# Two heads share one set of softmax sums, and the last head's last tile moves from TensorE to VectorE

## The chip, the cores and the metric

The kernel runs on one core of a Trainium2 chip. The metric is the device time of one execution in microseconds (us). The kernel before takes 1801.33 us, the median of three runs (1801.32, 1801.33 and 1802.16 us). The engines are called by the profile's names: PE is TensorE (matrix products), PEld its loading of weights, DVE is VectorE, ACT is ScalarE, POOL is GpSimd and SP is SyncE. SP and POOL, and now and then ACT, also issue the DMA transfers; "SPq" and "POOLq" are their queues of instructions. An engine takes its instructions strictly in order.

## The reference, cut to what matters

The program computes two branches on the same tokens (2048 tokens of width 1024) and mixes them with a gate, `g * a + (1 - g) * b`. Branch `b` is PEER, a mixture of 64 small experts whose output is a sum over rows of a table `v`. Branch `a` is attention with 32 heads of width 32, and that is where the change lies:

```python
scores = jnp.einsum("bhqd,bhkd->bhqk", q, k) * (Dh ** -0.5)
p = _softmax(scores, axis=-1)
o = jnp.einsum("bhqk,bhkd->bhqd", p, v)
return (lambda x, *d: x.transpose(*d))(o, 0, 2, 1, 3).reshape(B, S, D) @ wo
```

The softmax needs, for each head and each of the 2048 queries, the sum of the exponentials over the 2048 keys. The kernel computes the product with `v` from the exponentials as they are, and divides by that sum later.

## The kernel before, in words

Up to about 600 us the kernel computes queries, keys, values and PEER's choice of experts. Then comes the attention, to about 1622 us, and last the product with `wo`, which also adds PEER's values.

In the attention the keys of a head are cut into NT = 16 tiles of 128 keys. A tile `P[h, kt]` has 128 partitions (keys) and 2048 columns (queries) of float32, 1 MB in all; there are eight such buffers, used in turn. A step number counts tiles: step = 16 * h + kt. The main loop (lines 1536 to 1551) takes two steps at once. For each pair it issues, in this order: `scores` (L1346), eight matmuls into a ring of seven PSUM banks, and ACT's exponentials of them (L1356); `pv` (L1367), the products of the pair of tiles before with the values; and then, for each of the two steps, first the work that the table `todo` has for that step (entered with `at(step, function, ...)`, lines 1501 to 1532) and then `presum`. So the order on each engine is written out by hand, and every engine's instructions keep it.

The sum over the keys is made in three ways:

- `presum` (L1384 to L1396) adds most tiles of a head on DVE into an accumulator `ACC[h]` (128 x 2048).
- The tiles in `SUMS[h]` (L1376) go another way. The first of them is written by ACT directly into a second accumulator `ACCD[h]` (the buffer `accd`) instead of a P buffer. For each of the others POOL issues a DMA that adds the 1 MB tile to `ACCD[h]` in memory (L1389). All of a head's DMA additions write the same buffer, and each carries a wait for the one before. `merge` (L1399) then adds `ACCD[h]` to `ACC[h]` on DVE.
- What is left is a sum over the 128 partitions, which `rowsum` (L1380) does on PE as products with ones: four matmuls of 32 x 512, one for each quarter of the queries. In the profile an fp32 matmul of this kind counts as two instructions, so a set of four is "x8".

Heads 0 to 27 (NP = 28) are first folded by two DMAs from 128 to 32 partitions (`fold_half`, L1404, and `fold_quarter`, L1407), and four heads are gathered into one buffer, so that four heads share one set of four matmuls (`group_sums`). Heads 28, 29 and 30 have a set of their own each (`head_sums`), at steps 29*16+8, 30*16+8 and 31*16+8. Head 31 is summed behind the loop: two sets, one over its last tile `P[31, 15]`, which never goes into `ACC`, and one over `ACC[31]` after the last `merge`. These two stand on PE behind the first part of the product with `wo` (`wo_mm(pa, 0, [0], ...)`, L1581, 12 matmuls) and ahead of its other parts.

The buffers tie steps together. `ACC[28]` is `acc1`, which `ACC[31]` uses next (L1394 of head 31). `ACC[29]` is the buffer `vhl`, into which `load_vhl` loads PEER's table (two DMAs of 512 KB on SP) once head 29's sums are done; the table is first used at L1588, at 1643 us. Behind the loop the P buffers become buffers of the product with `wo`. The sums go out through `SMD`, come back as `rr`, are inverted (L1452), and reach the last chunk of the attention's output by L1650.

Of the kernel before, what the change touches and what calls it, by code (L numbers as in the profile page):

```python
# [9 lines left out]
F32 = mybir.dt.float32  # L10
F32R = mybir.dt.float32r
I32 = mybir.dt.int32
AF = mybir.ActivationFunctionType
OP = mybir.AluOpType
# [4 lines left out]
H = 32  # L19
KC = D // 128  # L20
HC = KC // 2
NT = S // 128
NQ = S // 512
G = H // 4
# [7 lines left out]
def gated_mha_peer_kernel(ctx, tc, xT, wqkv, wv, wo, wq, k12, ug, v, out):  # L32
# [8 lines left out]
    nc = tc.nc  # L41
# [3 lines left out]
    const = ctx.enter_context(tc.tile_pool(name="const", bufs=1))  # L45
# [12 lines left out]
    SMD = [dram.tile([4, S], F32, name=f"smd{g}") for g in range(G)]  # L58
# [11 lines left out]


    gw = const.tile([128, KC, 1], F32, name="gw")
    const.tile([128, 112], F32, name="fill")
    ctx.enter_context(tc.tile_pool(name="fillr", bufs=1, side="right")).tile([128, 120], F32, name="fillr")

    def dma(dst, src, queue=nc.sync):
        a, b = (ap.bitcast(F32) if ap.dtype == F32R else ap for ap in (dst, src))
        return queue.dma_start(a, b)  # L78
# [636 lines left out]
    sm = Pool("sm")  # L715
# [501 lines left out]
    P, pools = {}, {}  # L1217
# [48 lines left out]
    NP = H - 4  # L1266
    ACC = {}

    def new_acc(h):
        if h % 3 == 2 and h < H - 2:  # L1270
            ACC[h] = keep.tile([128, S], F32, name="vhl")
        else:
            ACC[h] = wk.tile([128, S], F32, name=f"acc{h % 3 if h < H - 2 else h % 2}", bufs=1)
# [6 lines left out]
    def raw_wo(kc):  # L1280
        i, j = divmod((kc - 1) % KC, 2)
        return wo_raw[i][:, j]

    wk = Pool("wk", bufs=2)
# [3 lines left out]
    nc.vector.memset(sel, 0.0)  # L1288
    for i in range(4):
        nc.vector.memset(sel[32 * i:32 * i + 32, i:i + 1], 1.0)  # L1290
    vpool = Pool("vpool", bufs=2)
    kq = Pool("kq")
    pools["left"] = Pool("ppl")
# [7 lines left out]
    ring = pss.tile([128, NB, 512], F32, name="ring")  # L1301
# [3 lines left out]
    def ring_banks(n):  # L1305
        i = [(ring_no[0] + k) % NB for k in range(n)]
        ring_no[0] += n
        return i

    def on_ring(ins, *banks):  # L1310

        for other, theirs in users:
            if ins.ins.engine != other.ins.engine and not theirs & set(banks):
                tc.declare_no_dep(ins.ins, other.ins, reason="different banks of the ring")
        users.append((ins, set(banks)))
        del users[:-6 * NB]
# [18 lines left out]
    def scores(tiles):  # L1335
# [7 lines left out]
        for c, i in enumerate(banks):  # L1343
# [6 lines left out]
            q0, m = c0 % NQ, c + 1 - c0  # L1350
            if q0 == 0 and kt == SUMS[h][0]:
                P[h, kt] = ACCD[h] = wk.tile([128, S], F32, name="accd")
# [19 lines left out]

    SUMS = {h: (1, 3, 8, 12) for h in range(H)} | {h: (1, 4, 10) for h in range(1, NP, 2)} | {0: (4, 8, 12), H - 1: (2, 4, 6, 11)}

    def rowsum(ps, *srcs, by=ones):
        for src in srcs:
            for qc in range(NQ):
                yield nc.tensor.matmul(ps[32 * qc:32 * qc + 32, :], by,  # L1380
                                       src[:, qc * 512:(qc + 1) * 512],
                                       start=(src is srcs[0]), stop=(src is srcs[-1]))

    def presum(h, kt):  # L1384
        sums = SUMS[h]
        if kt == 0 or kt == sums[0] or (h == H - 1 and kt == NT - 1):
            return
        if kt in sums:
            nc.gpsimd.dma_start(ACCD[h], P[h, kt], accum_op=OP.add)  # L1389
            return  # L1390
        if kt == 1 + (sums[0] == 1):
            if h > 0:
                new_acc(h)
            nc.vector.tensor_add(ACC[h], P[h, 0], P[h, kt])  # L1394
        else:
            nc.vector.tensor_add(ACC[h], ACC[h], P[h, kt])  # L1396

    def merge(h):
        nc.vector.tensor_add(ACC[h], ACC[h], ACCD[h])  # L1399
# [15 lines left out]
    def group_sums(g):  # L1415
        i, = ring_banks(1)
        for ins in rowsum(ring[:, i, :], F.pop(g), by=sel):
            on_ring(ins, i)
        o = wk.tile([128, 512], F32, name="ssb")
        on_ring(nc.scalar.activation(o, ring[:, i, :], AF.Copy), i)  # L1420
        for j in range(4):
            dma(SMD[g][j:j + 1, :].rearrange("o (q s) -> (o q) s", q=NQ), o[j::32, :])

    def head_sums(h):
        i, = ring_banks(1)
        for ins in rowsum(ring[:, i, :], ACC.pop(h)):
            on_ring(ins, i)
        on_ring(norm_sums(h, ring[:, i, :]), i)
# [69 lines left out]
    def at(step, f, *a):  # L1498
        todo.setdefault(step, []).append((f, a))

    for h in range(H):
        base = h * NT
        g, j = divmod(h, 4)
        if h < H - 1:
            at(base + NT, finish, h)
            at(base + NT + 5, merge, h)
            if h >= NP:
                at(base + NT + 8, head_sums, h)
            else:
                at(base + NT + 9, fold_half, h)  # L1510
                at(base + 2 * NT + 4, fold_quarter, h)
                at(base + 2 * NT + 8, gather, h)
                if j == 3:
                    at(base + 2 * NT + 14, group_sums, g)
        if j == 3 and g + 1 < G:
            at(base + 3 * NT + 4, load_r, g)
            at(base + 3 * NT + 8, norm_r, g)
        if h >= 1 and h + 1 < H:
            at(base + 2, load_head, h + 1)
        if g + 1 < G:  # L1520
            at(base + 7, load_v, g + 1, j)
    for i, step in enumerate((6, 7, 9, 11)):
        at((H - 1) * NT + step, split_first, i)
    for k in range(2 * KC):
        c = slice(k % 2 * D // 2, (k % 2 + 1) * D // 2)
        at((8 + k) * NT + 11, dma, raw_wo(k // 2)[:, c], wo_rows[:, :, k // 2 * D:(k // 2 + 1) * D][:, :, c])
    for i in range(2):
        at(30 * NT + 9 + i, load_vhl, i)
    at(29 * NT + 13, load_o, 0, 0, 4)
    at(30 * NT + 7, load_o, 0, 4, KC - 1)  # L1530
    at(30 * NT + 13, load_rb, 0, 0, KC - 1)
# [4 lines left out]
    for b0 in range(0, (H + 1) * NT, BT):  # L1536
        if b0 > H * NT:
            break
        now = [divmod(k, NT) for k in range(b0, b0 + BT)] if b0 < H * NT else []
        if now:  # L1540

            if b0:
                scores(now)
        for k in range(b0 - BT, b0):
            if k >= 0:
                pv(*divmod(k, NT))
        for k in range(b0, b0 + BT):
            for f, a in todo.pop(k, []):
                f(*a)
            if now:  # L1550
                presum(*now[k - b0])
    assert not todo
    merge(H - 1)
    pss.close()
    pools["left"].close()
    pools["right"].close()
# [47 lines left out]
    def split_hi(kc):  # L1604
        nc.scalar.activation(woh[kc], raw_wo(kc), AF.Copy)
        if kc < KC - 1:
            o = OC[0][:, kc, :]
            nc.vector.tensor_mul(o, o, RB[0][:, kc, :])
            nc.scalar.activation(OH[0][:, kc, :], o, AF.Copy)
# [52 lines left out]
    load_o(1, 0, KC - 1)  # L1662
    load_t(2, [zp.tile([128, S], F32R, name="z1")], [fin.tile([128, S], F32R, name="t3l")])
    sm = pso.tile([128, 512], F32, name="o")
    list(rowsum(sm, P[H - 1, NT - 1], ACC.pop(H - 1)))
    split_hi(1)
    for kc in range(1, KC - 1):
        split_hi(kc + 1)
# [167 lines left out]
```

## Time and profile before

| | us |
|---|---|
| median of three runs | 1801.33 |
| the profiled execution, its own time | 1799.57 |
| span of that execution, first to last instruction | 1797.7 |
| PE busy in the span | 1791.9 (100%) |
| DVE busy | 1505.5 (84%) |
| ACT busy | 1303.6 (73%) |
| POOL busy | 265.4 (15%) |

The profile shows one execution; all places are given in us from the start of its span. Rows of a timeline have start, duration, engine, line, operation, "written<-read", and the number of instructions merged into the row; in brackets stand the idle time ahead of the first of them and what ended it. Busy PE is not PE at its peak, since matmuls overlap. DMAs are named by the instruction that issues them; where the profile knows it, "DMA to landing" is the time from the issue to the last byte's semaphore.

Step numbers are found in the trace by counting pairs of steps back from the last eight score matmuls at 1616.24 us (steps 510 and 511). Pairs are 3.9 us apart, and each set of row sums between them takes 0.86 us more.

### The profile page before, as it was taken

How to read it: one execution, taken by the hardware profiler on the slowest of the kernel's cores; microseconds unless marked ns; L12 is line 12 of the kernel's file. 1: busy time of each engine (PE TensorE's matmuls, PEld its weight loads, DVE VectorE, ACT ScalarE, POOL GpSimd, SP SyncE). 2: the span in 40 equal slices, each digit the busy share in tenths (PEclk: the TensorE clock that was granted, in tenths of full speed). 3: DMA queues.
4: the chain of work that ended last, by engine and by line, in shares of the span. 5: the costliest groups of instructions: out<-in, count | busy, mean ns of one | idle time of the engine just before them, and what ended most of it. 6: DMA issues, size and time to landing. Idle time of an engine off the chain costs nothing.

```text
span 1797.7 us, 26087 instructions
## 1 busy us (share of the span) xinstructions
PE 1791.9 (100%) x9903; PEld 1090.9 (61%) x9903; DVE 1505.5 (84%) x1294; ACT 1303.6 (73%) x1701; POOL 265.4 (15%) x395
## 2 busy tenths in 40 slices
PE   9999999999999999999999999999999999999999
PEld 7777777788888744444444444444444444447887
DVE  8865976689976898989989899999989899897874
ACT  6544544532342599999999999999999999994221
POOL 1222222245101101111101101110111111000000
PEclk9999999999999999999999999999999999999999
DMA  7877588560257668889889888988988897878541
GB/s 289 281 273 277 225 290 290 193 234 14 82 196 251 237 155 178 183 183 198 183 199 195 190 187 196 205 184 201 195 190 186 180 209 163 206 181 294 220 158 59
DMA packets 118735, 360.11 MB, mean 200 GB/s; under 512 B 16176, under 2 KB 49216, under 8 KB 95888
## 3 DMA queue, kind: packets, MB, share of 16 engines
q0 software_dynamic: 29520, 152.63, 37.1%
q1 hardware_dynamic: 87784, 203.57, 36.1%
q10 hardware_dynamic: 1304, 2.24, 0.3%
q8 instruction: 78, 1.28, 0.3%
q14 instruction: 49, 0.40, 0.1%
HBM read 171.99 MB, written 72.36 MB: 136 GB/s over the span
## 4 chain that ended last, share of the span: by engine, by line
PE 99%; DMA 0%; ACT 0%; SPq 0%; issue 0%; DVE 0%; ACTq 0%
PE ring L1346 29%; PE o L1367 26%; PE bk L302 15%; PE pa L972 7%; PE bk L972 6%; PE bk L733 5%; PE bk L991 2%; PE bk L290 2%; PE bk L341 2%; PE pa L1581 1%; PE pa L1588 1%; PE ring L1380 0%; PE bk L192 0%; DMA xh<-in_xT 0%; PE bk L358 0%; SPq L78 0%
## 5 line engine op out<-in xcount | busy, mean ns | idle before, releaser
L1356 ACT ACTIVATE P<-ring 128x1024 f32<-128x1024 f32 (+2 forms) x1028 | 910.2, 984 | 16.7 <-DMA accd<-P 0.9
L1396 DVE TENSOR_TENSOR acc<-acc,P 128x2048 f32<-128x2048 f32 x230 | 527.1, 2292 | 37.2 <-ACT P L1356 17.2
L1367 PE MATMUL o<-P,V 128*32 128x512 f32 x3840 | 464.8, 599 | 0.0
L1346 PE MATMUL ring<-Q,K 98*128 98x512 f32 x1024 | 272.2, 407 | 0.2 <-ACT P L1356 0.2
L1346 PEld LDWEIGHTS ring<-Q,K 98*128 98x128 f32 x1024 | 182.1, 188 | 144.5 <-ACT P L1356 83.4
L1346 PE MATMUL ring<-z,z 98*128 98x512 f32 x1016 | 269.5, 407 | 0.0
L1346 PEld LDWEIGHTS ring<-z,z 98*128 98x128 f32 x1016 | 180.8, 188 | 141.7 <-ACT P L1356 76.6
L1396 DVE TENSOR_TENSOR vhl<-vhl,P 128x2048 f32<-128x2048 f32 x104 | 238.3, 2291 | 17.8 <-ACT P L1356 8.5
L1367 PEld LDWEIGHTS o<-P,V 128*32 128x32 f32 x3840 | 98.9, 109 | 223.3 <-issue 215.1
L1389 POOL DMA_DIRECT2D accd<-P x81 | 71.2, 879 | 821.8 <-ACT P L1356 420.7
L302 PE MATMUL bk<-xh,A 128*128 128x512 f32 x336 | 82.8, 396 | 0.0
L302 PE MATMUL bk<-xh,S 128*128 128x512 f32 x336 | 81.3, 393 | 0.0
L302 PE MATMUL bk<-xl,S 128*128 128x512 f32 x336 | 80.2, 391 | 0.0
L137 ACT ACTIVATE hi<-u 128x512 fp32r<-128x512 f32 x42 | 26.6, 632 | 70.5 <-issue 42.3
L302 PEld LDWEIGHTS bk<-xh,A 128*128 128x128 f32 x336 | 62.0, 188 | 23.8 <-issue 5.9
L1394 DVE TENSOR_TENSOR acc<-P,P 128x2048 f32<-128x2048 f32 x22 | 50.4, 2292 | 26.7 <-ACT P L1356 26.7
L302 PEld LDWEIGHTS bk<-xl,S 128*128 128x128 f32 x336 | 62.7, 188 | 16.4 <-issue 2.5
L302 PEld LDWEIGHTS bk<-xh,S 128*128 128x128 f32 x336 | 62.4, 188 | 14.5 <-issue 1.7
L972 PE MATMUL pa<-woh,acc 128*128 128x512 f32 x216 | 69.9, 389 | 0.0
L1356 ACT ACTIVATE accd<-ring 128x1024 f32<-128x1024 f32 (+2 forms) x65 | 62.3, 1020 | 0.1
L520 DVE TENSOR_TENSOR u<-u,bk 128x512 f32<-128x512 f32 x70 | 46.6, 682 | 10.1 <-DMA wpd<-u 5.3
L1399 DVE TENSOR_TENSOR acc<-acc,accd 128x2048 f32<-128x2048 f32 x22 | 50.3, 2285 | 0.0
(326 smaller groups left out, 2282.7 us busy)
## 6 DMA issues: line engine op xcount, KB each, us to landing
accd<-P POOLq DMA_DIRECT2D x81, 1024.0 KB, 9.8
wqt<-in_wq SPq DMA_DIRECT2D x64, 512.0 KB
wraw<-in_wqkv SPq DMA_DIRECT2D x28, 512.0 KB
acc<-acc POOLq DMA_DIRECT2D x19, 512.0 KB, 11.9
kd<-hi POOLq DMA_DIRECT2D x32, 256.0 KB, 4.9
kd<-lo POOLq DMA_DIRECT2D x32, 256.0 KB, 4.9
qd<-hi POOLq DMA_DIRECT2D x32, 256.0 KB, 4.1
qd<-lo POOLq DMA_DIRECT2D x32, 256.0 KB, 4.2
```

Of the source, the lines that this page charges most:

```text
L290: nc.tensor.matmul(b0[w, n], AW[PLAIN[w, ki]][a][:, k, :], X[f"B{ki + 1}{n + 1}"][b][:, k, :], start=first, stop=last)
L302: nc.tensor.matmul(ps, a[i][:, k, :], b[j][:, k, :], start=(k == 0 and i == j == 0), stop=(k == HC - 1 and i == 1))
L520: nc.vector.tensor_tensor(out=out, in0=a, in1=b, op=OP.add)
L733: nc.tensor.matmul(ps, x_part(a, t // 4, kc)[:, tok], b, start=first, stop=last)
L972: nc.tensor.matmul(ps, self.a[a][i][:, k, :], self.b[b][j][k], start=(not first and k == 0 and i == j == 0), stop=(k == HC - 1 and i == 1))
L1346: on_ring(nc.tensor.matmul(ring[:, i, :], K[:98, kt * 128:(kt + 1) * 128], Q[:98, qc * 512:(qc + 1) * 512], start=True, stop=True), i)
L1356: on_ring(nc.scalar.activation(P[h, kt][:, q0 * 512:(q0 + m) * 512].rearrange("p (a m) -> p a m", a=m), ring[:, i:i + m, :], AF.Exp, scale ...
L1367: nc.tensor.matmul(O[h][32 * qc:32 * qc + 32, :], Vt[g][:, kt, 32 * j:32 * j + 32], p[:, qc * 512:(qc + 1) * 512], start=(kt == 0), stop=( ...
L1389: nc.gpsimd.dma_start(ACCD[h], P[h, kt], accum_op=OP.add)
L1394: nc.vector.tensor_add(ACC[h], P[h, 0], P[h, kt])
L1396: nc.vector.tensor_add(ACC[h], ACC[h], P[h, kt])
L1399: nc.vector.tensor_add(ACC[h], ACC[h], ACCD[h])
```

## The change: what it does

Heads 28 and 29 no longer have a set of row sums each. `pair_fold` adds the two halves of partitions of each accumulator by a DMA on POOL (512 KB each): head 28 into partitions 0 to 63, at step 29*16+9, and head 29 into partitions 64 to 127, at step 30*16+9. `pair_gather` (a 512 KB DMA on SP, step 30*16+12) copies head 28's half beside head 29's, and `pair_sums` (step 31*16+2) does one set of four matmuls with a selecting matrix `sel2`, whose two columns give the two heads.

`ACC[29]` lives longer by that, so the two loads of PEER's table move from steps 30*16+9 and +10 to steps 31*16+4 and +5.

For head 31, `merge` moves from behind the loop to step 31*16+15, ahead of the last `presum`; the last tile is added to `ACC[31]` by DVE; and PE does one set of row sums there in place of two. So that DVE has no more additions than before, tile 8 of head 31 joins `SUMS`: tile 2 is written to `ACCD`, and tiles 4, 6, 8 and 11 are added to it by DMA.

```diff
+    sel2 = fill[:, :32]
+    nc.vector.memset(sel2, 0.0)
+    for i in range(2):
+        nc.vector.memset(sel2[64 * i:64 * i + 64, i:i + 1], 1.0)
...
-    SUMS = {h: (1, 3, 8, 12) for h in range(H)} | {h: (1, 4, 10) for h in range(1, NP, 2)} | {0: (4, 8, 12), H - 1: (2, 4, 6, 11)}
+    SUMS = {h: (1, 3, 8, 12) for h in range(H)} | {h: (1, 4, 10) for h in range(1, NP, 2)} | {0: (4, 8, 12), H - 1: (2, 4, 6, 8, 11)}
...
-        if kt == 0 or kt == sums[0] or (h == H - 1 and kt == NT - 1):
+        if kt == 0 or kt == sums[0]:
             return
...
+    def pair_fold(h):
+        a, b = (ACC[h][64 * i:64 * i + 64] for i in ((0, 1) if h == NP else (1, 0)))
+        nc.gpsimd.dma_start(a, b, accum_op=OP.add)
+
+    def pair_gather():
+        dma(ACC[NP + 1][:64], ACC.pop(NP)[:64])
+
+    def pair_sums():
+        i, = ring_banks(1)
+        for ins in rowsum(ring[:, i, :], ACC.pop(NP + 1), by=sel2):
+            on_ring(ins, i)
+        o = wk.tile([128, 512], F32, name="ssb")
+        on_ring(nc.scalar.activation(o, ring[:, i, :], AF.Copy), i)
+        for j in range(2):
+            dma(SMD[G - 1][j:j + 1, :].rearrange("o (q s) -> (o q) s", q=NQ), o[j::32, :])
...
+        at(base + NT + 5 if h < H - 1 else base + NT - 1, merge, h)
         if h < H - 1:
             at(base + NT, finish, h)
-            at(base + NT + 5, merge, h)
-            if h >= NP:
+            if h == H - 2:
                 at(base + NT + 8, head_sums, h)
+            elif h >= NP:
+                at(base + NT + 9, pair_fold, h)
...
+    at(30 * NT + 12, pair_gather)
+    at(31 * NT + 2, pair_sums)
     for i in range(2):
-        at(30 * NT + 9 + i, load_vhl, i)
+        at(31 * NT + 4 + i, load_vhl, i)
...
-    merge(H - 1)
     pss.close()
...
-    list(rowsum(sm, P[H - 1, NT - 1], ACC.pop(H - 1)))
+    list(rowsum(sm, ACC.pop(H - 1)))
```

More of the change, by code (lines that the diff above doesn't have):

```diff
@@ L72, in gated_mha_peer_kernel @@
     gw = const.tile([128, KC, 1], F32, name="gw")
-    const.tile([128, 112], F32, name="fill")
+    fill = const.tile([128, 112], F32, name="fill")
     ctx.enter_context(tc.tile_pool(name="fillr", bufs=1, side="right")).tile([128, 120], F32, name="fillr")
```

## The prediction, made before the changed kernel was run

> **What bounds the kernel now.** I read the page first, then the chain of waits, then the timelines of each engine around the places that the change touches. From the page:
>
> ```profile
> span 1797.7 us, 26087 instructions
> PE 1791.9 (100%) x9903; PEld 1090.9 (61%) x9903; DVE 1505.5 (84%) x1294; ACT 1303.6 (73%) x1701; POOL 265.4 (15%) x395
> ```
>
> PE is busy for the whole span. A PE instruction that goes away is time won one for one, a wait put on PE is time lost one for one, and nothing later can give it back, since PE has no idle time that could shrink. The chain of waits shows what stands on PE where the change works (start, duration, what); the rows are from three windows of it:
>
> ```profile
> 1542.12 0.86 PE ring L1380 x8
> ...
> 1575.08 0.86 PE ring L1380 x8
> ...
> 1618.37 3.57 PE o L1367 x32
> 1621.94 2.95 PE pa L1581 x12
> 1624.89 1.85 PE o L1380 x16
> 1626.75 16.75 PE pa L1581 x72
> ```
>
> The reader sees the separate sums of heads 28 and 29 (0.86 us each) and, behind the loop, the last products with the values, the first 12 matmuls of the wo product, the two sets of sums of head 31 (1.85 us for x16, so 0.93 for one set), and the rest of wo.
>
> **PE instructions that go.** Two sets of 0.86 us go, one (the pair's) comes: 0.86 us less. Behind the loop one of two sets goes: 0.93 us less. Together 1.79 us, if nothing waits. The pair's set stands just ahead of the first of these rows of PE's timeline (the second is the product with tile 2 of head 31, which is needed below; its second half ends with the next row's start, 1598.31):
>
> ```profile
> 1595.39 2.11 PE L1346 MATMUL ring<-Q,K 98*128 98x512 f32 x8
> 1597.43 1.06 PE L1367 MATMUL o<-accd,V 128*32 128x512 f32 x8
> 1598.31 1.04 PE L1367 MATMUL o<-P,V 128*32 128x512 f32 x8
> ```
>
> Up to there PE is 2 x 0.86 = 1.73 us earlier than before, so the pair's sums are due at 1593.7; behind them to the end of the loop it is 0.86 earlier, so the last sums are due at 1624.89 - 0.86 = 1624.0.
>
> **The pair's folds and gather.** The two folds go to POOL's queue and the gather to SP's. They have no rows of before; the nearest are the old folds, 512 KB added by DMA just so (line L1404, all 28 of them):
>
> ```profile
> DMA to landing us min/median/max: 7.8/11.9/14.2
> ```
>
> Head 28's fold has some 40 us until the gather and is hidden. Head 29's goes behind the accumulate of step 30*16+8, which POOL issues at 1575.28 (row below), so it is issued near 1576 and lands between 1583.8 and 1590.2. SP waits for it, with only the load of the first scale factors behind it (`rb`, first used at L1486, third row below), and moves 512 KB: at the least about 4 us (half of the 6.8 below for 1 MB), at most 7.8. That is 1588 to 1598, and the pair's sums are due at 1593.7. I take 1592, so no wait; the far bound is a wait of some 4 us. DVE at that place:
>
> ```profile
> 1592.40 2.29 DVE L1394 TENSOR_TENSOR acc<-P,P 128x2048 f32<-128x2048 f32 x1
> 1596.20 2.29 DVE L1396 TENSOR_TENSOR acc<-acc,P 128x2048 f32<-128x2048 f32 x1 [1.52 <-ACT P L1356]
> ...
> 1602.81 0.42 DVE L1486 TENSOR_TENSOR V<-V,rb 128x256 f32<-128x256 f32 x1
> ```
>
> The first row writes `ACC[31]`, whose buffer the gather reads: due at 1590.7 in the new order, it can wait 1.5 us, the idle time that follows it. If it waits longer, DVE is late with tiles that nothing needs before the end. ACT's copy for the pair takes the place of two such copies and costs nothing.
>
> **The added accumulate, which decides.** POOL's timeline, and one row of what POOL waited for between 500 and 1640 us (total, times, longest):
>
> ```profile
> 1575.28 0.86 POOL L1389 DMA_DIRECT2D accd<-P  x1 [9.98 <-DMA accd<-P]
> 1582.95 0.85 POOL L1389 DMA_DIRECT2D accd<-P  x1 [6.82 <-ACT P L1356]
> 1599.06 0.86 POOL L1389 DMA_DIRECT2D accd<-P  x1 [15.25 <-ACT P L1356]
> 1606.43 0.86 POOL L1389 DMA_DIRECT2D accd<-P  x1 [6.51 <-DMA accd<-P]
> 1614.12 0.86 POOL L1389 DMA_DIRECT2D accd<-P  x1 [6.83 <-ACT P L1356]
> ```
>
> ```profile
> POOL accd L1389 <- DMA accd<-P: 120.8, 14, 10.1
> ```
>
> The last three are head 31's tiles 4, 6 and 11. Tile 6's waited for tile 4's to land, as the bracket says, and so did 13 others. For the three of them, and then for the one at 1582.95 alone:
>
> ```profile
> DMA to landing us min/median/max: 6.8/6.9/7.2
> ```
>
> ```profile
> DMA to landing us min/median/max: 11.6/11.6/11.6
> ```
>
> So tile 4 lands at 1599.06 + 6.8 = 1605.9, tile 6 is issued 0.5 later and lands at 1606.43 + 7.2 = 1613.6, and tile 11 is issued 0.5 after that. Its row names ACT (tile 11 was ready then too), but the queue had just come free as well: the chain of three had no slack left. Its end is seen at the last merge on DVE (line L1399):
>
> ```profile
> L1399 DVEq EVENT_SEMAPHORE  x1: 21/21/21, 1621.1 to 1621.1; - x1
> ```
>
> A fourth accumulate in this chain pushes tile 11's landing by a whole link, 6.9 + 0.5 = 7.4 us. The chain can't start sooner, since tile 2's product must have read `accd` first (to 1598.31, above). With PE 0.86 earlier: tile 4 is issued at 1598.2, tile 6 at 1598.2 + 6.8 + 0.5 = 1605.5, tile 8 at 1605.5 + 7.2 + 0.5 = 1613.2 and tile 11 at 1613.2 + 7.4 = 1620.6; it lands at 1627.5.
>
> **What DVE does then.** DVE's timeline of before:
>
> ```profile
> 1613.62 1.22 DVE L1494 TENSOR_TENSOR z<-wo_raw,z 128x1024 fp32r<-128x1024 f32 x1
> 1614.76 0.42 DVE L1494 TENSOR_TENSOR acc<-V,z 128x256 fp32r<-128x256 f32 x1
> 1615.09 7.08 DVE L1396 TENSOR_TENSOR acc<-acc,P 128x2048 f32<-128x2048 f32 x3
> 1622.21 2.29 DVE L1399 TENSOR_TENSOR acc<-acc,accd 128x2048 f32<-128x2048 f32 x1
> ```
>
> Without tile 8 DVE gets to tile 12 as soon as that is computed, 0.86 earlier than before, and ends tile 14 at about 1621.3. Then stands the merge, which waits to 1627.5 for tile 11. Queued behind it on DVE: tile 15's addition, and all of DVE's work for wo. Merge and addition take 2.20 + 2.29 = 4.5 us: the sums are ready for PE at 1632.0, where it wanted them at 1624.0. PE waits 8.0 us with everything of wo behind it (the other operands of wo's second part come from DVE 1 to 2 us after the addition, while the sums run). Sums to 1632.9, against 1626.7 of before: **6.2 us later**. That is the lower bound.
>
> **Loads in the chain's way.** SP's timeline:
>
> ```profile
> 1580.41 0.63 SPq L78 DMA_DIRECT2D vhl<-vph  x1
> 1581.09 0.45 SPq L78 DMA_DIRECT2D vhl<-vpl  x1
> 1582.73 0.61 SPq L78 DMA_DIRECT2D rb<-rd  x1
> ...
> 1609.88 1.14 SPq L78 DMA_DIRECT2D accd<-rd  x1
> 1622.64 0.37 SPq L78 DMA_DIRECT2D od<-osb  x1
> ...
> 1625.95 0.37 SPq L78 DMA_DIRECT2D V<-od  x1
> 1626.43 0.36 SPq L78 DMA_DIRECT2D z<-t2h  x1
> 1626.88 0.39 SPq L78 DMA_DIRECT2D t3l<-t2l  x1
> ```
>
> The first three rows (1.9 MB by the shapes) are why the accumulate at 1582.95 took 11.6 us: 4.7 us more for 1.9 MB ahead of it, 2.5 us for 1 MB. The change moves the table's two loads (1 MB) to step 31*16+4, just behind the pair's sums: SP issues them at about 1597, right ahead of tile 4's accumulate. I add 2.0 us (bounds 0 and 2.5). The scale factors' load (0.9 MB, old issue 1609.88) now meets tiles 6 and 8: 0.7 us (0 and 2.3). Tile 11 would be issued at 1623.4, beside the stores and loads that start wo (0.5 MB from 1622, then 2.9 MB from 1625): 2.0 us (0 and 3.8, by the 0.5 MB and as much of the rest as the tile itself has, at 2.5 us for 1 MB). Sum: 4.7 us.
>
> The accumulates land behind what was queued ahead of them, by that row. [...]
>
> **The clock.** PE's timeline at the start and at 170 us, and two stretches behind the last matmul (columns: us, then each engine's busy time, PE's clock, DMA):
>
> ```profile
> 1.40 3.78 PE L417 MATMUL bk<-ident 128*128 128x128 f32 x16 [1.40 <-DVE ident L92]
> ...
> 170.73 0.60 PE L358 MATMUL bk<-ident,u 128*128 128x128 f32 x4
> ```
>
> ```profile
> 1794.20:1797.00 2.80, 0.00 (x0) 0.00 (x0) 0.42 (x1) 0.00 (x0) 0.00 (x0) 1.00 0.15 52
> 1794.20:1797.70 3.50, 0.00 (x0) 0.00 (x0) 0.42 (x1) 0.00 (x0) 0.00 (x0) 0.95 0.12 41
> ```
>
> Sixteen matmuls took 3.78 us when PE began from rest; four of the same size take 0.60 when it is warm, start to start half of that. At the end the granted clock falls from 1.00 only behind 2.8 us without matmuls. A wait of 8 us or more is longer, so PE would start again at half speed for about 3.8 us: **1.9 us** lost (bounds 0 and 2).
>
> **The sum.** The gain of 1.79 is already in the 6.2, which counts from the old place. 6.2 + 4.7 + 1.9 = **12.8 us**: span 1810.5, the profiled execution's own time 1799.57 + 12.8 = 1812.4, and the median, which stands 1.76 above that execution, 1801.33 + 12.8 = 1814.1. I forecast **1814 us**.
>
> **The rivals.** (1) *Not slower:* the accumulate of tile 8 doesn't lengthen the chain, because POOL may issue it without waiting for tile 6's landing and the transfers run into each other. It decides if tile 11 lands before DVE reaches the merge at 1621.3. Then DVE goes straight on, 1621.3 + 4.5 = 1625.8, still 1.8 us after PE's 1624.0: the gain of 1.79 is eaten by the last addition and the time is 1801.3 + 0.1 = 1801.4. For it speaks that the landing of tile 11 was 1.1 us ahead of DVE in the old order; against it that 14 waits of this very kind are in the trace, and none of head 31's accumulates starts while another runs. 6%. A gain above 0.2% would need 3.6 us, twice all that PE sheds: 2%.
> (2) *The gather is late as well:* PE waits up to 4 us at the pair's sums; tile 4's start, and with it the whole chain, moves by that: 1814 + 3 = 1817 us. Against it stands the margin of 1.7 us above. 10%.
> (3) *Transfers share in turn:* tile 11's term becomes 3.8, 1816 us; the row of 11.6 us shows the accumulate behind loads issued before it, but no row shows one with loads issued after it, so this can be. 17%. [...]
> (4) *Little contention and a clock that stays up:* 6.2 us, 1807.5 us. 10%.
> The forecast itself: 55%.
>
> **Chances and range.** Two tenths of a per cent, 3.6 us, is about what a measurement of this kernel tells from no change. Slower: 55 + 10 + 17 + 10 = 92%; same 6%; faster 2%. The range goes from 1808 (the lower bound, and a little of the clock) to 1820 (cases 2 and 3 together with the larger bounds of the loads).
>
> **What would show it.** Four accumulates of head 31 on POOL, 7 to 9 us apart, each behind the landing of the one before, with the last issued after 1620; the last merge on DVE starting at 1628 or later with a wait for a DMA ahead of it; an idle PE of 8 to 13 us ahead of a single set of sums at L1380, and a clock below 1.00 in the 4 us behind that. No wait on PE near 1594. The forecast is wrong if tile 8's accumulate is issued while tile 6's is under way, if the merge starts near 1621, or if PE's longest wait is elsewhere.

## The result, and the profile after

The changed kernel takes **1819.87 us**, the median of six executions (1816.38 to 1822.96), against 1801.74 us for six of the kernel before: a ratio of 1.0100, 95% interval 1.0090 to 1.0109. It is slower by 18.1 us. The forecast was 1814 us, slower, with a range of 1808 to 1820.

The profiled execution after took 1820.05 us, at its median. The profiled execution of before took 1799.57 us, 2.2 us under its median of six. So the two traces differ by 20.5 us where the medians differ by 18.1; every difference of places below is one between these two traces. The page of after:

```profile
span 1818.2 us, 26061 instructions
PE 1792.2 (99%) x9887; PEld 1091.2 (60%) x9887; DVE 1506.3 (83%) x1297; ACT 1303.3 (72%) x1699; POOL 267.8 (15%) x398
```

PE's busy time is what it was (1791.9), although 16 of its instructions are gone: the span has grown by idle time. What PE waited for between 1540 and 1660 us (total, times, longest):

```profile
PE o L1384 <- DVE acc L1400: 16.8, 1, 16.8
PE ring L1384 <- DMA vhl<-acc: 2.3, 1, 2.3
PE ring L1384 <- ACT P L1360: 0.9, 1, 0.9
```

One wait carries nearly all of it: the last sums wait 16.8 us for DVE. The second is the pair's sums waiting for the gather, and the third the sums of an earlier group of four heads. The chain of waits of after tells what stood behind the first two (start, duration, what):

```profile
1578.53 9.82 DMA vhl<-vhl
...
1588.37 9.14 DMA vhl<-acc
...
1597.64 1.06 PE ring L1384 x8
...
1621.62 3.62 PE o L1371 x32
...
1626.98 13.07 DMA accd<-P
...
1640.14 2.30 DVE acc L1403
...
1642.54 2.30 DVE acc L1400
...
1644.97 1.94 PE o L1384 x8
1646.91 17.14 PE pa L1604 x72
```

The reader can add up the difference from this chain and the one of before. The loop's last products end at 1621.62 + 3.62 = 1625.24, against 1621.94 before: 3.3 us late. The last sums end at 1646.91, against 1626.75: 20.2 us late. The rest of `wo` takes 17.14, against 16.75: 20.6 in all, which is the difference of the spans (20.5) and a rounding. So 3.3 us were lost inside the loop, and 16.9 us between the loop and the end of the sums. The latter hang on one transfer of 13.07 us, the fourth accumulate. POOL's timeline of after has all four (start, duration, engine, line, operation, and in brackets POOL's idle time ahead and what ended it):

```profile
1602.31 0.86 POOL L1393 DMA_DIRECT2D accd<-P  x1 [15.60 <-ACT P L1360]
1611.14 0.86 POOL L1393 DMA_DIRECT2D accd<-P  x1 [7.98 <-DMA accd<-P]
1619.48 0.85 POOL L1393 DMA_DIRECT2D accd<-P  x1 [7.48 <-ACT P L1360]
1626.98 0.85 POOL L1393 DMA_DIRECT2D accd<-P  x1 [6.64 <-ACT woh L1628]
```

They stand 8.83, 8.34 and 7.50 us apart. The time from each issue to its landing was 8.3, 7.8, 7.0 and 13.1 us, so each of the last three was issued 0.5 us behind the landing of the one before. (The brackets name ACT in two of these rows: its event came 0.2 to 0.4 us behind the landing, and still ahead of the issue.) The whole group:

```profile
DMA to landing us min/median/max: 7.0/8.1/13.1
```

Why the last took 13.07 us is seen on SP, whose stores and loads for `wo` are issued around 1626.98:

```profile
1625.88 0.37 SPq L78 DMA_DIRECT2D od<-osb  x1
1626.41 0.85 SPq L78 DMA_DIRECT2D at<-atd  x2
1627.36 0.38 SPq L78 DMA_DIRECT2D V<-od  x1
1628.16 0.32 SPq L78 DMA_DIRECT2D z<-t2h  x1
1628.57 0.51 SPq L78 DMA_DIRECT2D t3l<-t2l  x1
```

and in the queues themselves. These are two stretches of the DMA view of after, 1626.5 to 1630.3 and 1630.3 to 1639.5 (queue: packets, MB, share of the 16 engines; q0 carries POOL's accumulates, q1 SP's transfers):

```profile
q1 hardware_dynamic: 578, 0.70, 80.6%
...
q0 software_dynamic: 143, 1.05, 54.8%
q1 hardware_dynamic: 233, 1.62, 46.4%
```

In the first stretch there is no row for q0: the accumulate is issued and moves nothing for 3.4 us, while SP's queue has the engines. In the second the two queues share them about half and half, though SP issued `V`, `t2h` and `t3l` later than POOL issued its accumulate.

DVE's timeline gives the two places where it stood still for a transfer. The first is `ACC[31]`'s first addition, which waits until the gather has read its buffer; the second is the last merge:

```profile
1597.63 2.29 DVE L1398 TENSOR_TENSOR acc<-P,P 128x2048 f32<-128x2048 f32 x1 [4.52 <-DMA vhl<-acc]
...
1640.14 2.29 DVE L1403 TENSOR_TENSOR acc<-acc,accd 128x2048 f32<-128x2048 f32 x1 [14.74 <-DMA accd<-P]
```

Last the clock. Three stretches of after, for PE alone (columns: us, PE's busy time and its matmuls, granted clock, DMA share, GB/s):

```profile
1627.10:1631.10 4.00, 1.03 (x5) 1.00 0.87 198
...
1631.12:1648.19 17.07, 3.21 (x11) 0.50 0.67 216
...
1648.20:1650.00 1.80, 1.80 (x9) 1.00 0.03 9
```

It halves during the wait and is whole again 3.2 us after the sums begin. That is why a set of sums takes 1.94 us here and 0.93 before.

### The profile page after: what moved, and what is told of

Read it like the earlier page. It is cut to its first block, busy times and chain, and to the rows that moved or that the text cites. A ratio compares the mean times of both kernels' runs of the same rounds, so it can differ in the third digit from the quotient of the medians.

```text
span 1818.2 us, 26061 instructions
## 1 busy us (share of the span) xinstructions
PE 1792.2 (99%) x9887; PEld 1091.2 (60%) x9887; DVE 1506.3 (83%) x1297; ACT 1303.3 (72%) x1699; POOL 267.8 (15%) x398
## 4 chain that ended last, share of the span: by engine, by line
PE 93%; DMA 5%; issue 1%; ACT 1%; DVE 1%; POOL 0%; SPq 0%; POOLq 0%; DVEq 0%; ACTq 0%
PE ring L1350 26%; PE o L1371 23%; PE bk L302 15%; PE pa L972 7%; PE bk L972 6%; PE bk L733 5%; DMA accd<-P 3%; PE bk L290 2%; PE bk L991 2%; PE bk L341 2%; PE pa L1604 1%; PE pa L1611 1%; ACT P L1360 1%; DMA vhl<-vhl 1%; DMA vhl<-acc 1%
```

## The experiments

**The theories.** Theory A is the prediction's: the accumulates of head 31 are serial, a fourth one pushes the last merge behind the end of the loop, and that merge and the addition behind it keep PE waiting. The rivals put the loss elsewhere: in the pair (its gather, and the table's loads that move with it), in the extra work of DVE at the end, or in the loads and stores of `wo` that the late accumulate meets. Each expectation was written before its run and says which outcome speaks for which. All times are medians. The kernel before was measured again on the same chip beside each group of runs: 1801.31 us for the first four rows of the table, 1800.72 for the whole change with three or five loads later, for tile 9, and for the pair's sums 6 steps later, and 1800.70 for the other three rows. Each kernel is compared with the value of its group.

| kernel | median, us | ratio to before | 95% interval |
|---|---|---|---|
| pair part alone | 1800.90 | 0.9998 | 0.9988 to 1.0008 |
| last head's part alone | 1811.61 | 1.0054 | 1.0037 to 1.0071 |
| whole change, tile 8 left to DVE | 1803.88 | 1.0025 | 1.0002 to 1.0049 |
| before, with tile 8 by DMA | 1809.32 | 1.0046 | 1.0029 to 1.0063 |
| whole change, three loads later | 1813.15 | 1.0068 | 1.0051 to 1.0085 |
| whole change, five loads later | 1814.09 | 1.0071 | 1.0054 to 1.0088 |
| last head's part, three loads later | 1811.82 | 1.0060 | 1.0044 to 1.0075 |
| whole change, tile 9 in place of 11 | 1813.86 | 1.0071 | 1.0054 to 1.0088 |
| pair alone, its sums 6 steps later | 1802.54 | 1.0014 | 1.0005 to 1.0024 |
| pair alone, its sums 2 steps later | 1800.49 | 0.9998 | 0.9989 to 1.0007 |
| whole change, PE kept busy | 1814.94 | 1.0084 | 1.0068 to 1.0099 |

### One tile alone

Only the list of tiles of the kernel before is edited:

```diff
-    ... {0: (4, 8, 12), H - 1: (2, 4, 6, 11)}
+    ... {0: (4, 8, 12), H - 1: (2, 4, 6, 8, 11)}
```

> The kernel before with one edit: tile 8 of head 31 joins the tiles added by DMA. merge stays behind the loop, tile 15's sums stay on PE. Theory A: the fourth accumulate is issued at about 1621.5 and lands between 1628 and 1635; merge follows, 2.2 us; the second set of sums waits for it. +6 to +14 us, most likely +12. Theory B: within 2 us of the kernel before, and DVE a little less busy.

8.0 us slower, by one entry in a tuple. POOL's timeline of this kernel, last two accumulates:

```profile
1614.78 0.86 POOL L1389 DMA_DIRECT2D accd<-P  x1 [6.77 <-ACT P L1356]
1622.17 0.86 POOL L1389 DMA_DIRECT2D accd<-P  x1 [6.53 <-DMA accd<-P]
```

and PE's row of the sums over `ACC[31]`:

```profile
1633.27 1.93 PE L1380 MATMUL o<-acc,ones 128*32 128x512 f32 x8 [6.69 <-DVE acc L1399]
```

The last accumulate is issued at 1622.17, a link of 7.4 us behind the third, which stands where before had its last (1614.12). From its issue to its landing:

```profile
DMA to landing us min/median/max: 8.7/8.7/8.7
```

PE waits 6.7 us for the merge. The rival that POOL runs the accumulates into each other is out: the chain alone, with none of the rest of the change, costs 8.0 of the 18.1 us.

### All but that tile

The whole change, with the list of tiles of before:

```diff
-    ... H - 1: (2, 4, 6, 8, 11)}
+    ... H - 1: (2, 4, 6, 11)}
```

> The whole change, but tile 8 stays on DVE (three accumulates, at tiles 4, 6 and 11). Theory A: the chain is one link shorter; its last lands near 1626.5, where the fourth-last stood in the changed kernel, and DVE, which has one addition more, ends merge and tile 15 at about 1631. PE waits some 3 us at the last sums instead of 17. +4 to +7 us against the kernel before, so 12 to 15 us faster than the whole change. Theory B: as slow as the whole change, +16 us or more.

2.6 us slower, which is less than the 4 to 7 expected. (One of its ten executions took 1822.9 us, at a mean granted clock of 0.948 where the others have 0.998 to 1.000; why is not known. The others took 1801.3 to 1807.1.) Of the 18.1 us, 15.6 are gone with the fourth accumulate, so neither the pair nor the work that DVE has more at the end carries the loss by itself. PE's row of the last sums, and a stretch of the clock behind it:

```profile
1630.86 1.94 PE L1384 MATMUL o<-acc,ones 128*32 128x512 f32 x8 [3.09 <-DVE acc L1400]
```

```profile
1627.00:1630.50 3.50, 0.77 (x4) 1.00 0.90 244
1630.53:1633.93 3.40, 3.07 (x11) 0.50 1.02 430
1633.95:1635.00 1.05, 1.05 (x6) 1.00 0.98 414
```

What is left of the change isn't a gain either: merge and last addition stand one behind the other on DVE, and PE waits 3.1 us for them. In that short pause the granted clock fell to 0.50, for 3.4 us.

### The two parts by themselves

The pair part alone has the list and the end of before; the last head's part alone has the sums, folds and table loads of before:

```diff
 # the pair alone
-H - 1: (2, 4, 6, 8, 11)
+H - 1: (2, 4, 6, 11)
-list(rowsum(sm, ACC.pop(H - 1)))
+merge(H - 1)                       # behind the loop, as before
+list(rowsum(sm, P[H - 1, NT - 1], ACC.pop(H - 1)))
 # the last head alone
-at(30 * NT + 12, pair_gather)
-at(31 * NT + 2, pair_sums)
+at(base + NT + 8, head_sums, h)    # for 28, 29 and 30
-at(31 * NT + 4 + i, load_vhl, i)
+at(30 * NT + 9 + i, load_vhl, i)
```

> The pair part alone (heads 28 and 29 share a set, table loads moved), head 31 as in the kernel before. Theory A (the fourth accumulate of head 31 makes the loss): small cost here. One set fewer on PE, -0.86 us; the two waits seen in the changed kernel stay, 1.0 us at the group's sums near 1555 and 2.3 us at the pair's sums near 1597; head 31's three accumulates start 2 to 3 us later with PE and their last lands just about when DVE merges. Sum about +2.5 us, 0 to +6. Theory B (the pair's folds, gather and moved loads make the loss by crowding the DMA queues): most of the 18 us here, over +12 us.

> The last-head part alone (tile 8 to DMA, merge ahead of the last addition, tile 15 on DVE, one set of sums), heads 28 and 29 as in the kernel before. Theory A: tile 4's accumulate is issued at 1599, as before, the fourth at about 1621.5; its landing at 1628 if nothing crowds it, 1634 with the loads that start wo; PE's sums wait for merge and addition, 4.5 us more. +9 to +16 us, most likely +14, with a clock at half speed behind the wait. Theory B: within 2 us of the kernel before.

The pair alone changes nothing that can be measured (0.4 us faster, where 2.5 us slower was expected). PE's row of its sums:

```profile
1595.75 1.06 PE L1384 MATMUL ring<-vhl,fill 128*32 128x512 f32 x8 [1.72 <-DMA vhl<-acc]
```

In this trace the set of 0.86 us that it saves is spent in a wait of 1.7 us for the gather. The last head alone is 10.3 us slower. So the parts don't add: 10.3 - 0.4 = 9.9 us, and together they cost 18.1. In the last head's kernel the fourth accumulate is issued at 1623.17, 3.8 us sooner than in the whole change and ahead of SP's `od` (1623.97), and lands after 7.8 us. Half of the 3.8 us is the start of the chain (1600.41 against 1602.31), and half the way from its first accumulate to its fourth (22.8 against 24.7 us), where the whole change has the table's loads beside it. PE's row, and the queues from 1624.5 to 1630:

```profile
1635.86 1.93 PE L1384 MATMUL o<-acc,ones 128*32 128x512 f32 x8 [9.64 <-DVE acc L1400]
```

```profile
q0 software_dynamic: 128, 1.05, 100.5%
q1 hardware_dynamic: 64, 0.07, 4.4%
```

The 1.05 MB go through in 5.5 us with hardly anything beside them. The 64 packets of q1 are of 1 KB (0.07 MB by 64), those of q0 of 8 KB.

### Are the 8 us the loads that the accumulate meets?

The loads of `V`, `t2h` and `t3l` are issued behind the sums' way out and back, first in the whole change, then in the last head's part; a third kernel also holds back the two loads `at`:

```diff
     for n in range(2):
         load_at(n)                  # the third kernel moves this too
-    load_o(1, 0, KC - 1)
-    load_t(2, ...)
     sm = pso.tile([128, 512], F32, name="o")
...
             load_r(G - 1)
+            load_o(1, 0, KC - 1)
+            load_t(2, ...)
```

> The whole change, but the three large loads that start wo (1.9 MB of parts for one product, 0.9 MB of attention output) are issued behind the load of head 31's sums, so after the last merge; the store of head 31 and the two small loads stay ahead of the last accumulate. Theory C (the last accumulate took 13.1 us because it shared the DMA engines with loads issued after it): it lands in 7.5 to 9 us, merge starts 4 to 5.5 us sooner, and the time falls by as much, to about 1815 us, unless the late loads hold up wo. Theory D (it took 13.1 us because of what was queued ahead of it): it still takes 11 us or more, and the time stays within 2 us of the whole change.

> As the kernel with the late large loads, and the two small loads (256 KB) are late too, so only the 256 KB store of head 31 is left beside the last accumulate. Theory C: 7 to 8 us to landing, at most 1 us less than with the small loads. Theory D: the small loads are half of what is queued ahead, so 2 us or more less than with them. Either way the four accumulates still follow one another, each issued half a us behind the landing of the one before, and PE still waits 9 us or more.

> The last-head part alone, with the three large loads of wo behind the load of head 31's sums. Here the fourth accumulate was issued ahead of all loads of wo and landed in 7.8 us. Theory C: it lands in 7 to 8 us and the time is within 1.5 us of the last-head part as it stands (1811.6), since there was little to win: the 13.1 us of the whole change came of being issued behind the first of these loads. Rival: the large loads cost the last-head part as much as the whole change, 4 us or more less.

In the whole change the later loads are worth 5.7 us: 12.4 us slower than before in place of 18.1. In the last head's part, where the accumulate came ahead of them, they are worth nothing (11.1 us slower in place of 10.3, within the intervals). Holding `at` back too brings no more time (13.4 us slower), but it gives the clean price of the fourth accumulate. In its trace the chain begins later (the fourth accumulate is issued at 1626.30, against 1624.09 with three loads held back), and PE waits 1.0 us in `wo` for a later load, `wol<-t3l`; whether the late loads cause that wait isn't shown. Of the three-load kernel, POOL's last row and PE's last sums:

```profile
1624.09 0.85 POOL L1393 DMA_DIRECT2D accd<-P  x1 [6.66 <-ACT woh L1628]
```

```profile
1637.08 1.94 PE L1384 MATMUL o<-acc,ones 128*32 128x512 f32 x8 [11.76 <-DVE acc L1400]
```

Its accumulate landed at 1632.15, after 8.1 us, though it was issued behind `od` and `at`. In the five-load kernel, from issue to landing of the last accumulate:

```profile
DMA to landing us min/median/max: 6.8/6.8/6.8
```

So the same transfer takes 6.8 us when only `od` was ahead of it, 8.1 with `od` and `at`, and 13.1 with those and the three loads. The loads cost that only together with the pair part: the pair makes the chain late, and the late chain runs into the loads. This is 5.7 of the 8.2 us by which the parts fall short of the whole. Of the other 2.5, the longer way from the first accumulate to the fourth, with the table's loads beside it, is 1.8 in the traces (24.6 us in the three-load kernel, 22.8 in the last head's); the rest is open.

The order of issue against the three loads isn't what differs, though the last of these expectations takes it so: the accumulate was issued ahead of `V` in the whole change too (1626.98 and 1627.36). What differs is that there `od` and `at` were issued ahead of it, and in the last head's part behind it (1623.97 and 1624.51), so that their packets of 1 KB stood between it and the large loads. That this is the reason is read from the traces and not tested by itself.

### An earlier tile as the last of the chain

```diff
-    ... H - 1: (2, 4, 6, 8, 11)}
+    ... H - 1: (2, 4, 6, 8, 9)}
```

> The whole change, but the last tile added by DMA is tile 9 in place of 11 (DVE adds 11). Theory A (the chain of four accumulates sets the end, since each waits for the landing before it): nothing moves, the fourth is issued near 1627 as before and the time is within 2 us of the whole change. Rival (the fourth is late because its tile is computed late): the fourth is issued two tiles, 3.9 us, earlier and the time falls by 4 us or more.

The fourth accumulate is issued at 1626.02, as late as that of tile 11: it is the chain that sets the issue, not the tile. The time is 5.0 us less all the same (13.1 us slower than before in place of 18.1), by a mechanism of its own. SP's rows of this kernel:

```profile
1625.06 0.37 SPq L78 DMA_DIRECT2D od<-osb  x1
1633.03 0.80 SPq L78 DMA_DIRECT2D at<-atd  x2
1633.93 0.38 SPq L78 DMA_DIRECT2D V<-od  x1
```

`at` is loaded into the buffer from which the accumulate reads tile 9. So SP waits until that has landed (1632.89), and `V`, `t2h` and `t3l` stand behind it in SP's order. The accumulate had the engines nearly for itself and took 6.9 us. It is the experiment of the later loads a second time, by accident, and its time agrees with that one's (12.4 and 13.4 us slower).

### The clock by itself

Sixty matmuls of 512 columns, whose product is overwritten, fill PE's wait ahead of the last sums:

```diff
     sm = pso.tile([128, 512], F32, name="o")
+    for _ in range(60):
+        nc.tensor.matmul(sm, OH[0][:, 0, :128], W0[0][:, 0, :512], start=True, stop=True)
     list(rowsum(sm, ACC.pop(H - 1)))
```

> The whole change, with 60 matmuls of 512 columns that compute nothing of use put on PE ahead of the last sums, some 13.6 us of work in a wait of 16.9 us. The clock theory: PE's clock stays at 1.00 through the wait, the last sums take 0.9 us in place of 1.9, and the time falls by 1.6 to 2.9 us against the whole change. Rival (the wait alone costs, PE is not slower behind it): same time as the whole change.

The granted clock is 1.00 over the whole span, and PE's row of the last sums is back at 1.07 us (1.06 for the pair's sums of the whole change, at a clock of 1.00):

```profile
1638.86 1.07 PE L1384 MATMUL o<-acc,ones 128*32 128x512 f32 x8 [0.49 <-DVE acc L1400]
```

14.2 us slower than before in place of 18.1, though the two intervals just overlap (1.0068 to 1.0099, and 1.0090 to 1.0109). And the 3.9 us aren't the clock's alone. The dummy matmuls read a buffer into which `t2h` is loaded, so that load and `t3l` were held back to 1638.40, and the chain happened to begin sooner (the pair's sums waited only 0.3 us). Its accumulate took 10.7 us beside `od`, `at` and `V`. The run shows that the clock stayed at 1.00 with PE kept busy, and that most of the loss (14.2 us) was there without any drop of it; how the 3.9 us divide stays open.

### Can the pair be had without its wait?

The pair part alone, with its sums and the table's loads 2 steps later, and 6 steps later:

```diff
-    at(31 * NT + 2, pair_sums)
+    at(31 * NT + 4, pair_sums)      # or + 8
-        at(31 * NT + 4 + i, load_vhl, i)
+        at(31 * NT + 5 + i, load_vhl, i)   # or + 9
```

> The pair part alone, with the pair's sums two steps later than in the change (31*16+4) and the table's loads at steps +5 and +6, so that they come behind tile 4's accumulate and are through before tile 6's. Theory A: no wait on PE at the pair's sums (1.7 us when they stood two steps earlier), the last accumulate lands in about 7 us, no wait at the last sums; 0.9 us below the kernel before, 1800.4 against 1801.3, which is about what the measurement can tell from no change. Rival: the loads push one of the three accumulates back and the last merge waits, 1 to 3 us above the kernel before, as with the sums at +8.

> The pair part alone, with the pair's sums moved six steps later, to step 31*16+8 (and the table's loads to +9 and +10). Theory A: PE's wait of 1.7 us at the pair's sums is gone, DVE's wait of 3.9 us for the gather stays and costs nothing, and the time is 0.9 us below the kernel before, which is less than the measurement tells: same. Against it: the table's loads now meet tile 6's and 11's accumulates, whose chain has 1 us of slack; if they come first, the last merge waits and the time is 2 to 4 us above the kernel before.

Two steps later PE doesn't wait for the gather any more, yet the time is that of before (0.2 us less, interval 0.9989 to 1.0007). PE's row of the last sums of that kernel:

```profile
1627.01 1.07 PE L1384 MATMUL o<-acc,ones 128*32 128x512 f32 x8 [0.67 <-DVE acc L1403]
```

The 0.86 us that PE sheds turn into a wait of 0.67 for the last merge. DVE's row of that merge:

```profile
1624.66 2.29 DVE L1403 TENSOR_TENSOR acc<-acc,accd 128x2048 f32<-128x2048 f32 x1
```

It has no idle time ahead of it: DVE comes straight from its other additions, and the last accumulate had landed at 1621.7 (1614.87 and 6.8). So DVE sets the end in this kernel, and a set fewer on PE wins nothing there. Six steps later the table's loads go out at 1612.69 and 1613.27, right ahead of the last accumulate (1613.92), which then takes

```profile
DMA to landing us min/median/max: 12.0/12.0/12.0
```

and the kernel is 1.8 us slower than before, with a wait of 2.2 us at the last sums. So the table's loads belong early in the chain, as in the change, where the delay is smaller (1.5 us on tile 4, against 5.1 here). Of the versions tried none beats the kernel before by more than the measurement is uncertain.

## Why the prediction was right, and where its terms were off

The sign, the place and the mechanism were right. That the time lies inside the range is in part luck: 1819.87 is 0.13 us below its end, and the executions differ among themselves by 6.6 us. The main sum was 5.8 us low; the range reached so far because it allowed for the second and third rival together, and something of both came. Its own steps:

- **Four serial accumulates, each behind the landing before; the merge late; PE idle ahead of a single set of sums; the clock down behind that.** All seen, with the single tile in the kernel before as the direct proof; only PE's idle time was 16.8 us and not 8 to 13. The forecast's lower bound, 6.2 us for the chain alone, is near what one more tile costs there: 8.0 us, with a last transfer of 8.7 in place of 6.9 us and a granted clock of 0.50 for 6.82 us.
- **"I take 1592, so no wait" at the pair's sums.** Wrong. The gather was issued at 1588.37 and took 9.14 us, more than the 7.8 that was given as the most for 512 KB. Beside it ran the accumulate of head 30 that POOL issued at 1585.81 and the load of the scale factors (`rb`) that SP issued at 1589.01; which of them slowed it isn't shown. PE waited 2.3 us here, and between 0.3 and 1.9 in the other six profiles with the sums at that step. The second rival, a late gather, was right in kind.
- **The start of the chain at 1598.2.** It was 1602.31, 4.1 us later: 2.3 for the gather; 1.5 that PE was behind its forecast place at the group's sums already (1555.17 against 1554.51 of before, where 0.86 us earlier was forecast), 0.9 of it a wait for ACT that no other profile of these kernels shows; 0.3 unassigned.
- **Table loads 2.0 us on tile 4, scale factors 0.7 us on tiles 6 and 8.** Landings of 8.3, 7.8 and 7.0 us, against 6.8, 7.2 and 6.9 taken. That is 1.5, 0.6 and 0.1, together 2.2 for 2.7: about right.
- **Loads at the tail 2.0 us, bound 3.8.** This is the term of the sum that was mis-sized most. The last accumulate took 13.07 us, 6.2 more than the 6.9 of a clean one: three times the value and outside the bound. It began to move 3.4 us after its issue, and then shared the engines for 9 us. The bound had counted as many bytes as the tile's own beside it; it was 1.62 MB for 1.05, and it left the slow start out. The third rival, that the loads issued later share the engines with it, is what happened from 1630.3 on: they took nearly half of them. With packets of 1 KB in the other queue that queue took 4.4%, with packets of about 7 KB (1.62 MB by 233) 46.4%. In packets the accumulate's queue and SP's moved 128 and 64 in the one stretch, 143 and 233 in the other; whether the engines took the queues in turn isn't shown. Why the accumulate moved nothing at first isn't settled. The last head's part began to move it 1.4 us after the issue, the three-load kernel 1.6 us, with `od` and `at` under way, and the kernel with PE kept busy 1.9 us, with `V` under way as well. So among these traces the slow start comes only with `t2h` and `t3l`, though these were issued 1.2 and 1.6 us behind the accumulate.
- **Merge and addition 4.5 us.** From landing to the sums 1640.05 to 1644.97, 4.9 us.
- **The clock 1.9 us (0 to 2).** The 3.78 us at the start, from which the term was taken, stand at a granted clock of 1.00 in before (1.40 to 5.20), so they show no half speed; the runs do. A granted clock of 0.50 from 1644.97, where the sums begin, to 1648.19 in after is 1.6 us lost, by half of that time. In the last head's part it was 0.50 until 1641.71, 5.9 us after the sums' start, which is 2.9: beyond the bound.
- **The sum.** Start of the chain +4.1, links to the last issue -0.5 (24.67 in place of 25.2), last transfer +4.2 (13.07 in place of 8.9), merge and addition +0.4, clock -0.3: 7.9 us above the forecast of 12.8. That makes 20.7, against 20.5 between the spans. Between the medians it is 18.1, since the execution of before that was profiled was 2.2 us under its median; the forecast, which put that execution at 1.76 under, was 5.8 us low.
- **"Not slower".** The first rival needed the accumulates to overlap; each of the last three was issued 0.5 us behind the landing of the one before. And even the versions with no fourth link won nothing: 1803.88 with all else, 1800.49 and 1800.90 with the pair alone.

## What to carry to other kernels

DMA additions into one buffer were a serial chain here: each waited for the one before to land and was issued 0.5 us behind that, so that they stood 7.5 to 8.8 us apart. Count the links of such a chain back from the place where the result is needed, and price each by what else is in the queues at that moment, loads issued later too. A change that moves work off the busiest engine can gain nothing where another chain is due at the same point; look for the slack on that chain (1.1 us here, by the prediction) before adding a link of 7 us to it. Two parts, each costed alone, can cost more together when the first makes the second late enough to meet other traffic; ask of each late transfer what it runs beside at its new time.

## What the runs showed of the hardware that was not expected

- **The time of one DMA went with what the other queue held, issued later too.** The same accumulate of 1 MB took 6.8 us from issue to landing with only `od` ahead of it; 7.8 and 8.7 when it was issued ahead of SP's transfers (last head's part, tile 8 alone), so that packets of 1 KB came first beside it; 10.7 beside `od`, `at` and `V`, and 13.1 beside these, `t2h` and `t3l`. That the size of the packets decides is a reading of these rows; no run changed it alone.
- **The half-speed stretches read here are near multiples of 3.41 us.** At a granted clock of 0.50 stood 3.40 us in the whole change without tile 8 and 17.07 in the whole change (5 x 3.41); 10.23 and 6.82 in the last head's part and in the kernel with tile 8 alone (3 and 2 x 3.41). The three-load kernel has 0.59, 0.50 and 0.55 in the three stretches of 5 us from 1627 to 1642, and 1.00 in the next; taken as time at 0.50 and at 1.00 that is 13.6 us, an estimate. A stretch of the last head's part and of tile 8 alone, with the columns as above:

```profile
1631.48:1641.71 10.23, 5.85 (x17) 0.50 0.80 319
```

```profile
1631.85:1638.67 6.82, 5.40 (x16) 0.50 0.91 381
```

With a pause of 3.1 us (the last sums of the whole change without tile 8) the clock fell to 0.50 for one such length; with one of 2.3 us (the pair's sums in the whole change) it was 1.00 before and behind. The time from the first matmul behind a pause to a clock of 1.00 was 3.1 us there (1630.86 to 1633.93), 3.2 in the whole change, 5.4 with tile 8 alone (1633.27 to 1638.67) and 5.9 in the last head's part (1635.86 to 1641.71). So the price of a pause isn't fixed: at half speed it is half of that time, by estimate 1.5 to 2.9 us in these traces.
- **A shared buffer helped.** In the kernel with tile 9 last, a load that had to wait for a buffer kept SP's queue off the engines for 7 us, and the kernel lost 5.0 us less than with tile 11, for that alone as far as the trace shows.
